# Two attentions on one core: the layout is told later landings for stacked keys and log-sum rows

## Chip, cores, metric

One Trainium2 chip, one core. The time is device microseconds of one execution; the number shown is the median of several executions. One execution was also taken by the hardware profiler, and the views quoted below come from that one.

## What is computed

Two attention blocks, each with its own input, weights and output projection, on sequences of 2048 positions with 1024 features, 32 heads of 32. B looks back over a dense window of 256 keys; A over 8 keys at distance 2. Cut to what matters:

```python
def _A_ref(x, wqkv, wo):          # W, dil = 8, 2
    q, k, v = split_heads(x @ wqkv)
    idx = pos[:, None] - arange(8)[None, :] * 2
    logits = einsum("bhsd,bhswd->bhsw", q, gather(k, idx)) * Dh ** -0.5
    attn = softmax(where(idx >= 0, logits, -1e9))
    return merge(einsum("bhsw,bhswd->bhsd", attn, gather(v, idx))) @ wo

def _B_ref(x, wqkv, wo):          # W = 256
    q, k, v = split_heads(x @ wqkv)
    scores = einsum("bhqd,bhkd->bhqk", q, k) * Dh ** -0.5
    mask = (i - j >= 0) & (i - j < 256)
    return merge(einsum("bhqk,bhkd->bhqd", softmax(where(mask, scores, -1e9)), v)) @ wo

return concatenate([A, B], axis=-1)
```

The positions of A are sorted into even and odd ones before the launch, so that its 8 keys at distance 2 are 8 neighbours.

## The kernel before

**Units and head groups.** The work is cut into 8 units of 512 positions: four of B (dense), then four of A (window). Each unit has 8 head groups of four heads, so there are 64 head groups, which the code numbers hg. For each head group the kernel computes queries and keys (L412, three matmuls of 512 columns for each of 8 slices of the contraction), for each pair of head groups values (L464, 256 columns), and for each unit the output projection (L510). Every projection is three matmuls per slice because each factor is split into a high and a low part; a weight tile arrives by a 512 KB load (L137, on GpSimd's queue after the first few) and DVE splits it with one cast (L163) and two subtractions (L171).

**Attention of a head group.** The query and key tiles are evacuated from PSUM in a high part (ACT, L349) and a low part (DVE, L353), into one of three `nat` buffers. SyncE copies both parts, stacked three deep, into `qst` and `kst` (L373: two copies of the high part and one of the low for keys), of which there are two each. The *first pass* (L681, 16 matmuls) makes the scores, DVE takes the row maxima (L686), ACT the sum of exponentials (L691). From maxima and sums the *log-sum* of each row is made (L704 to L712), turned with one matmul (L720), copied out of PSUM (L724) and put by a small DMA into two extra rows of `qst` (L727). With these rows the *second pass* (L763 in dense units, L566 in window units) makes scores that are already normalised in the exponent; ACT exponentiates, masks are applied, and L810 or L607 multiplies with the values. When the last second-pass matmul of a head group has been put in, the head group after the next may be stacked into the same `qst` and `kst` (`free_keys`, L629).

**The order is a plan.** The kernel is written out instruction by instruction in the order in which it was planned, and each engine runs its own instructions in that order. The plan is made by a small model, the class `Clock` (L35), while the kernel is being written out. It keeps a time for each engine and for the DMA, with constants for each step. A copy by SyncE, for example, starts `LEAD` = 1.34 us after its issue, moves for the first and ends after the second number of its kind in `MOVE` (`copy`: 1.18 and 0.56; `rows`: 0.37 and 0.56), and transfers follow one another in one lane.

There are four lists of items for TensorE: `aux` (the turn of the log-sums), `twos` (second pass and values), `ones` (first pass) and `gemm` (all projections). The loop at the end (L872) asks the next item of each list when it is ready, takes the one that can start first, with that order of lists where several are ready, and advances TensorE's clock by the item's cost. A projection item is one slice of the contraction: three matmuls of 512 columns, or six of 256. What an item triggers on other engines is put in when the clock reaches its time, so the order on ACT, DVE, GpSimd and SyncE follows from the same walk.

The two times that matter here are `done["stack"]`, the time at which the clock has the low keys of a head group stacked (L361), read by the first pass's items alone (L734), and `h["rows"]`, at which it has the log-sum rows in place (L728), read by the second pass's items alone (L793 and L620). On the chip these instructions wait on the semaphores of the real transfers, whatever the clock said.

Of the kernel before, what the change touches and what calls it, by code (L numbers as in the profile page):

```python
# [21 lines left out]
NRAW, NP, NO, NS = 3, 768, 10, 4  # L22
POOL_BIAS = -99
MASK_BIAS = 0.2
VPARTS = ((0,2),(2,2),(4,2),(6,2))
V_SLOTS = {0: 0, 1: 1, 5: 2, 7: 3}
O_SLOTS = {2: (0, 1), 3: (2, 3), 4: (4, 5), 5: (6, 7)}
V0_SLOTS = {0:0,2:1,4:2,7:3}
NX, NST, NN = 9,1,3
TAIL, XAT = 4, 1  # L30
C1, C3, CG, CV = 0.108, 0.2, 0.231, 0.242
TERMS = ((0, 0), (0, 1), (1, 0))
# [148 lines left out]
def kernel(ctx, tc, xs, wqk, wv, wo, outs, units):  # L181
# [19 lines left out]
    ck = Clock()  # L201
# [28 lines left out]
    for p in plan:  # L230
# [3 lines left out]
        elif p[0] == "v":  # L234
            s0, n = VPARTS[p[2]]
            for g in range(n):
# [55 lines left out]
    pfree = [0.0]  # L292
    vbuf = [const.tile([P, 6, n * P], F32, name=f"vbuf{i}") for i, (_, n) in enumerate(VPARTS)]
    vpart = {s0 + i: (p, i * P) for p, (s0, n) in enumerate(VPARTS) for i in range(n)}
    halo = [[dram.tile([P, 2, 256], F32, name=f"halo{i}_{s}") for s in range(NG)] for i in range(2)]

    xt, xready, ot = {}, {}, {}
    done, waiting = {}, {}
# [30 lines left out]
    def latest(*ts):  # L329
        return None if any(t is None for t in ts) else max(ts)  # L330


    def qk_items(u, s):
        out = []
        dense, has_halo = units[u][2], units[u][3]
        buf = s % 2
        hg = u * NG + s

        def read_halo():
            w = 256 if dense else 128  # L340
            hb = halo[(u + 1) % 2][s]
            for r, a in enumerate((0, 1, 0)):
                nc.sync.dma_start(kst[buf][r:96:3, :, 256 - w:256].bitcast(F32), hb[:, a, 256 - w:])
                ck.copy("halo_in" if dense else "halo_few", ck.now)

        def evac(t, ps, bank):
            hl = natp.tile([P, 2, S], F32R, tag="nat", name="nat")
            sc = SCALE if t == 0 else 1.0
            nc.scalar.activation(hl[:, 0, :], ps, AF.Copy, scale=sc)  # L349
            r = ck.use("act", 0.485, ck.now + ck.SEM)  # L350

            def low():
                nc.vector.scalar_tensor_tensor(hl[:, 1, :], ps, sc, hl[:, 0, :].bitcast(F32), op0=ALU.mult,  # L353
                                               op1=ALU.subtract)
                e = ck.use("dve", 0.61, r)
                rg.give(bank, e)

                def stack():
                    e2 = place(1, e)
                    if t == 1:  # L360
                        done["stack"][u, s] = max(e2, h2["hi"])  # L361
                    if t == 1 and u + 1 < U and units[u + 1][3]:
                        nc.sync.dma_start(halo[u % 2][s], hl[:, :, 256:].bitcast(F32))
                        e2 = ck.copy("halo_out", e, ck.now)
                    done["nat"][hg, t] = max(e2, h2["hi"])

                later(stack)

            def place(part, e):
                dst, c = (qst[buf], 0) if t == 0 else (kst[buf], 256)  # L370
                for i, a in enumerate((0, 0, 1) if t == 0 else (0, 1, 0)):
                    if a == part:
                        nc.sync.dma_start(dst[i:96:3, :, c:c + S].bitcast(F32), hl[:, a, :].bitcast(F32))  # L373
                        e2 = ck.copy("copy", e, ck.now)
                return e2

            def stack_hi():
                if t == 0 and has_halo:
                    read_halo()
                h2["hi"] = place(0, r)  # L380

            def later(f):
                if hg < 2 or hg - 2 in done["second"]:
                    f()
                else:
                    waiting.setdefault(hg - 2, []).append(f)

            h2 = {}
            later(stack_hi)
            ck.defer(r, low)  # L390

        for t in range(2):
            h = {}

            def ready(k, t=t, h=h):
                if k == 0:
                    st.split_to(where["qk", u, s, t] + 1)
                    h["w"] = st.ready[where["qk", u, s, t]]
                    return latest(rg.when(), h["w"], xready[u][0])
                if k >= len(xready[u]):  # L400
                    return None
                if k == NK - 1 and 2 * hg + t >= NN:
                    n = done["nat"].get(divmod(2 * hg + t - NN, 2))
                    return n and max(xready[u][k], n - 0.6)
                return xready[u][k]

            def run(k, t=t, h=h):
                if k == 0:
                    h["ps"], h["b"] = rg.take()
                    h["w"], _ = st.get(where["qk", u, s, t])  # L410
                for i, (a, b) in enumerate(TERMS):
                    nc.tensor.matmul(h["ps"], h["w"][:, a, k * P:(k + 1) * P], xt[u][k][:, b, :],  # L412
                                     start=(k == 0 and i == 0), stop=(k == NK - 1 and i == 2))
                if k == 3 and st.items[min(where["qk", u, s, t] + 1, len(st.items) - 1)][0] != "x":
                    st.split_to(where["qk", u, s, t] + 2)

            def after(k, t=t, h=h):
                if k == NK - 1:
                    evac(t, h["ps"], h["b"])

            for k in range(NK):
                out.append((lambda k=k, ready=ready: ready(k), lambda k=k, run=run: run(k), 3 * CG,
                            lambda k=k, after=after: after(k)))
        return out
# [11 lines left out]
    def v_items(u, part):  # L436
# [3 lines left out]
        h = {}  # L440
        s0, ng = VPARTS[part]
        nb, per = ng, 4 // ng
# [92 lines left out]
    def x_items(u):  # L535
        xt[u], xready[u] = [], []

        def run(g):
            a, b = st.get(where["x", u, g])
            xt[u] += a  # L540
            xready[u] += b

        return [[(lambda: 0.0, lambda g=g: run(g), 0.0, lambda: None)] for g in range(4)]
# [112 lines left out]
    def attention(u, s):  # L656
# [6 lines left out]
        h = {"left": 16, "rows": None}  # L663
# [54 lines left out]
        def rows(hl):  # L718
            ps, bank = rs.take()
            nc.tensor.matmul(ps[0:32, 0:P], hl.rearrange("p a b -> p (a b)"), cst["ident"], start=True, stop=True)  # L720
            rt = small.tile([32, P], F32R, tag="rt", name="rt")

            def copy():
                nc.vector.tensor_copy(rt, ps[0:32, 0:P])  # L724
                e = ck.use("dve", 0.2, ck.now)
                rs.give(bank, e)
                nc.sync.dma_start(q[96:98, :, :].bitcast(F32), rt.bitcast(F32))  # L727
                h["rows"] = ck.copy("rows", e)  # L728

            return copy  # L730

# [14 lines left out]
        def keep(w, mask, n, m, step, base, chan, r):  # L746
            dur_p, dur_d = m * n / 960 + 0.13, m * n / 960 + 0.07
            if ck.ends("pool", dur_p, r) <= ck.ends("dve", dur_d, r, port=True) + MASK_BIAS:
                nc.gpsimd.affine_select(w, w, pattern=[[0, m], [step, n]], compare_op=ALU.is_ge, fill=0.0,  # L749
# [90 lines left out]
    for p in plan:  # L840
# [8 lines left out]
        elif p[0] == "v":  # L849
            new = v_items(p[1], p[2])  # L850
            if V_SLOTS.get(NG - 1) == p[2] and p[1] + 1 < U:
                m = 2 * VPARTS[p[2]][1]
                for g, x in reversed(list(enumerate(x_items(p[1] + 1)))):
# [89 lines left out]
```

## Time and profile before

| | |
|---|---|
| median of 3 runs | 1946.54 us (1946.42, 1946.54, 1950.07) |
| the profiled execution | 1951.22 us |
| its span, first to last instruction | 1949.5 us |
| mean granted TensorE clock | 0.995 |
| L412, query and key projection | 799.2 us busy, 3072 matmuls |
| L464, value projection | 411.8 us busy, 3072 matmuls |
| L510, output projection (one of its three forms) | 356.7 us busy, 1416 matmuls |
| L681, first pass | 232.6 us busy, 1024 matmuls |
| stack copies qst<-nat and kst<-nat | 192 each, 256 KB each |
| row copies qst<-rt | 64, 16 KB each |
| weight and input loads on GpSimd's queue | 126 + 64 + 62 + 28, 512 KB each |

Busy time of an engine is the union of its instructions' spans. A wait is idle time of an engine just before an instruction, put down to the semaphore that came last. The chain of waits is followed back from the last instruction. The timeline lists instructions of all engines in order of time, merged where they follow one another; its times are us from the span's start.

### The profile page before, as it was taken

How to read it: one execution, taken by the hardware profiler on the slowest of the kernel's cores; microseconds unless marked ns; L12 is line 12 of the kernel's file. 1: busy time of each engine (PE TensorE's matmuls, PEld its weight loads, DVE VectorE, ACT ScalarE, POOL GpSimd, SP SyncE). 2: the span in 40 equal slices, each digit the busy share in tenths (PEclk: the TensorE clock that was granted, in tenths of full speed). 3: DMA queues.
4: the chain of work that ended last, by engine and by line, in shares of the span. 5: the costliest groups of instructions: out<-in, count | busy, mean ns of one | idle time of the engine just before them, and what ended most of it. 6: DMA issues, size and time to landing. Idle time of an engine off the chain costs nothing. (4 is left out here: it accounts for less than half of the span.)

```text
span 1949.5 us, 35937 instructions
## 1 busy us (share of the span) xinstructions
PE 1904.4 (98%) x12608; PEld 1608.6 (83%) x12608; DVE 1261.6 (65%) x3733; ACT 960.6 (49%) x3136; POOL 375.8 (19%) x958
## 2 busy tenths in 40 slices
PE   8999999999999999999999999999999999999999
PEld 6787787788877888778878888888888788888887
DVE  6667566667666676666755667656676566765673
ACT  3555565655565656565655333433444343434441
POOL 1222222323332323232431001000010000000010
PEclk9999999999999999999999999999999999999999
DMA  6456555455545464555454556545564556546451
GB/s 200 131 141 174 134 147 166 136 150 174 144 141 166 133 185 120 144 147 144 134 147 118 173 164 188 157 133 169 148 182 128 169 158 174 167 130 176 138 157 66
DMA packets 136500, 294.90 MB, mean 151 GB/s; under 512 B 14464, under 2 KB 42112, under 8 KB 136320
## 3 DMA queue, kind: packets, MB, share of 16 engines
q1 hardware_dynamic: 85632, 124.82, 26.0%
q0 software_dynamic: 40320, 146.82, 23.2%
q10 hardware_dynamic: 10368, 20.98, 3.0%
q8 instruction: 100, 1.64, 0.4%
q14 instruction: 80, 0.66, 0.1%
HBM read 163.58 MB, written 27.26 MB: 98 GB/s over the span
## 5 line engine op out<-in xcount | busy, mean ns | idle before, releaser
L412 PE MATMUL g<-x,w 128*128 128x512 f32 x3072 | 799.2, 398 | 9.3 <-DVE w L163 9.0
L412 PEld LDWEIGHTS g<-x,w 128*128 128x128 f32 x3072 | 556.9, 189 | 109.3 <-DVE w L163 10.2
L691 ACT ACTIVATE s<-s,nm 128x384 f32<-128x384 f32 (+3 forms) x1024 | 452.2, 442 | 269.1 <-DVE nm L686 261.0
L464 PE MATMUL g<-w,x 128*128 128x256 f32 x3072 | 411.8, 285 | 0.0
L464 PEld LDWEIGHTS g<-w,x 128*128 128x128 f32 x3072 | 392.9, 192 | 2.0 <-issue 0.2
L686 DVE CUSTOM_DVE_ANT_0 s<-s,mask_d 128x384 f32<-128x384 f32 (+2 forms) x512 | 262.4, 555 | 188.5 <-PE s L681 187.7
L510 PE MATMUL g<-ot,w 128*128 128x512 f32 x1416 | 356.7, 396 | 2.7 <-ACT ot L644 2.3
L171 DVE TENSOR_TENSOR w<-raw,w 128x512 fp32r<-128x512 f32 x502 | 328.0, 695 | 8.7
L510 PEld LDWEIGHTS g<-ot,w 128*128 128x128 f32 x1416 | 258.5, 189 | 53.6 <-ACT ot L644 3.3
L749 POOL TENSOR_SCALAR_AFFINE_SELECT pbuf<-pbuf 128x128 f32<-128x128 f32 (+1 forms) x643 | 219.0, 372 | 296.9 <-ACT pbuf L770 295.8
L681 PE MATMUL s<-kst,qst 96*128 96x384 f32 (+3 forms) x1024 | 232.6, 302 | 15.7 <-DMA kst<-nat 9.7
L770 ACT ACTIVATE pbuf<-s 128x384 f32<-128x384 f32 (+2 forms) x480 | 201.9, 503 | 65.8 <-PE s L763 62.6
L681 PEld LDWEIGHTS s<-kst,qst 96*128 96x128 f32 x1024 | 178.4, 190 | 55.6 <-issue 18.2
L686 DVE CUSTOM_DVE_ANT_0 s<-s,mask_w 128x136 f32<-128x136 f32 (+1 forms) x512 | 142.0, 321 | 113.2 <-PE s L681 112.8
L691 ACT ACTIVATION_READ_ACCUMULATOR s<-s,nm 128x1 f32 x1024 | 209.9, 205 | 0.0
L349 ACT ACTIVATE nat<-g 128x512 fp32r<-128x512 f32 x128 | 76.6, 599 | 249.7 <-PE g L412 245.4
L137 POOL DMA_DIRECT2D raw<-wqk x126 | 68.0, 540 | 572.7 <-DVE w L171 218.2
L353 DVE SCALAR_TENSOR_TENSOR nat<-g,nat 128x512 fp32r<-128x512 f32 x128 | 88.3, 690 | 139.1 <-ACT nat L349 136.2
L163 DVE CAST w<-raw 128x1024 fp32r<-128x1024 f32 x251 | 173.1, 690 | 7.3 <-DMA raw<-wqk 7.3
L686 DVE DVE_READ_ACCUMULATOR2_ANT nm<- 128x1 f32 x1024 | 143.7, 140 | 0.0
L763 PEld LDWEIGHTS s<-qst,kst 98*128 98x128 f32 x704 | 109.0, 189 | 40.4 <-ACT s L691 19.6
L583 DVE TENSOR_TENSOR pbuf<-pbuf,keep_w 128x272 f32<-128x272 f32 (+1 forms) x224 | 95.5, 471 | 70.1 <-ACT pbuf L573 69.8
(53 smaller groups left out, 1071.3 us busy)
## 6 DMA issues: line engine op xcount, KB each, us to landing
raw<-wqk POOLq DMA_DIRECT2D x126, 512.0 KB, 3.7
qst<-nat SPq DMA_DIRECT2D x192, 256.0 KB
kst<-nat SPq DMA_DIRECT2D x192, 256.0 KB
raw<-wo POOLq DMA_DIRECT2D x64, 512.0 KB, 3.7
raw<-wv POOLq DMA_DIRECT2D x62, 512.0 KB, 3.7
raw<-xs POOLq DMA_DIRECT2D x28, 512.0 KB, 4.7
outs<-ost ACTq DMA_DIRECT2D x56, 256.0 KB
halo<-nat SPq DMA_DIRECT2D x40, 256.0 KB
```

The costliest lines, as they stand in the source:

```text
L163: nc.vector.tensor_copy(t[:, 0, :], raw)
L171: nc.vector.tensor_tensor(o, a, b, op=ALU.subtract)
L412: nc.tensor.matmul(h["ps"], h["w"][:, a, k * P:(k + 1) * P], xt[u][k][:, b, :], start=(k == 0 and i == 0), stop=(k == NK - 1 and i == 2))
L464: nc.tensor.matmul(ps, xt[u][k][:, a, p0:p0 + P], h["w"][:, c, k % kw], start=(k == 0 and i == 0 and r == 0), stop=(k == NK - 1 and i == 2 ...
L510: nc.tensor.matmul(h["ps"], w[:, a, c:c + P], ot[u, k][:, b, :], start=(k == 0 and i == 0), stop=(k == NK - 1 and i == 2))
L583: nc.vector.tensor_tensor(w, w, cst["keep_w"][:, None, :n].to_broadcast([P, pack, n]), op=ALU.min)
L681: nc.tensor.matmul(ps[:, :n], q[0:96, j, b * P:(b + 1) * P], kk[0:96, j, c0:c1], start=True, stop=True)
L686: nc.vector.tensor_tensor_reduce(ps[:, :n], ps[:, :n], mask[:, cut:full], scale=-1.0, scalar=BIG, op0=ALU.add, op1=ALU.min, accum_out=nm)
L691: nc.scalar.activation(ps[:, :n], ps[:, :n], AF.Exp, bias=nm, scale=-1.0, accum_out=sm)
L749: nc.gpsimd.affine_select(w, w, pattern=[[0, m], [step, n]], compare_op=ALU.is_ge, fill=0.0, base=base, channel_multiplier=chan)
L763: nc.tensor.matmul(ps[:, i * n:(i + 1) * n], kk[0:98, j, 256 + kb * P:256 + (kb + 1) * P], q[0:98, j, q0:q0 + n], start=True, stop=True)
L770: nc.scalar.activation(w, ps[:, :pack * n].rearrange("p (j n) -> p j n", j=pack), AF.Exp)
```

## The change

Two constants are added, and each is added to one of the two times. One other line differs in spacing only.

```diff
+ROWS_LATE, KEYS_LATE = .4, .5
...
-NX, NST, NN = 9,1,3
+NX, NST, NN = 9, 1, 3
@@ def stack():
                     e2 = place(1, e)
                     if t == 1:
-                        done["stack"][u, s] = max(e2, h2["hi"])
+                        done["stack"][u, s] = max(e2, h2["hi"]) + KEYS_LATE
                     if t == 1 and u + 1 < U and units[u + 1][3]:
@@ def copy():
                 nc.sync.dma_start(q[96:98, :, :].bitcast(F32), rt.bitcast(F32))
-                h["rows"] = ck.copy("rows", e)
+                h["rows"] = ck.copy("rows", e) + ROWS_LATE
```

The clock's own account of SyncE and of the DMA is not touched: only the time that the items are told is later. `done["nat"]`, which tells the projections when a `nat` buffer is free, keeps its value.

## Prediction

> **What bounds the kernel now.** I read the page first, for the engine that is never free, then TensorE's own waits, then the chain and the timelines around those waits, last the granted clock by stretch.
>
> ```profile
> PE 1904.4 (98%) x12608; PEld 1608.6 (83%) x12608; DVE 1261.6 (65%) x3733; ACT 960.6 (49%) x3136; POOL 375.8 (19%) x958
> PE g L412 8%; PE g L510 6%; PE g L464 4%; PE s L566 1%; PE s L681 1%; PE o L607 1%; DMA qst<-rt 0%; DMA kst<-nat 0%; PE s L510 0%; DVE w L171 0%; DVE w L163 0%; DVE pbuf L583 0%; DVE s L686 0%; ACT s L691 0%; ACT nat L349 0%
> ```
>
> TensorE is busy 98% of 1949.5 us and leads the chain; the only transfers in the chain are the two that the diff names: the stacking of low keys (kst<-nat) and the row values (qst<-rt). TensorE's queue is in order, so the time is its matmul work plus the moments in which its next instruction is not ready. Of the 1949.5 us only 45.1 are not busy, and nothing in this diff removes a matmul. So it can only act on that remainder.
>
> TensorE's waits, in us in total, times, longest:
>
> ```profile
> PE s L681 <- DMA kst<-nat: 9.7, 6, 2.5
> PE g L412 <- DVE w L163: 9.0, 3, 8.1
> PE s L763 <- DMA qst<-rt: 5.3, 4, 1.8
> PE s L681 <- ACT s L691: 5.2, 5, 1.6
> PE s L566 <- DMA qst<-rt: 3.0, 3, 1.7
> ```
>
> Thirteen waits end with a landing that the layout expected earlier: six of the first pass for keys (9.7 us), seven of the second pass for rows (5.3 + 3.0 = 8.3 us), 18.0 us together, 0.9% of the span. The 8.1 us of L412 is the start, before any head group. One row wait and one key wait of the same two groups stand in the chain of waits between 1505 and 1545 us (start, us, what):
>
> ```profile
> 1510.39 4.47 DMA qst<-rt
> 1514.86 0.14 issue
> 1515.00 1.34 PE s L566 x10
> 1516.34 0.75 PE g L412 x3
> ...
> 1529.85 6.46 DMA kst<-nat
> 1536.30 0.09 issue
> 1536.39 0.63 PE s L681 x4
> 1537.03 1.44 PE g L510 x6
> ```
>
> The row transfer took 4.47 us from its issue, where the layout's clock computes 1.34 + 0.37 + 0.56 = 2.27 us plus what it believes is ahead in the DMA. TensorE stood 1.69 us in front of L566 (timeline), although L412 matmuls came right after, so projection work was there to be put ahead. That is so at all thirteen: in TensorE's timeline projection matmuls stand directly before each wait and within a few instructions after it. Where nothing collides the same transfer needs far less: in the timeline at 1736 us the rows' cast ends at 1735.76 + 0.28 = 1736.04 and L566 starts at 1739.74 with no wait shown, 3.70 us later; at 1510 us it was 4.64 us, and there GpSimd had issued a 512 KB load 0.08 us behind the rows' issue.
>
> **What the diff changes.** No instruction, no tile, no transfer is added or taken out. Two numbers that the layout compares with its clock grow: done["stack"] by 0.5 us, read only by the first pass's items, and h["rows"] by 0.4 us, read only by the second pass's. The layout's own queues (SP's above all) don't get longer. An attention item that would be due stays back 0.4 or 0.5 us, and projection items go first if they are ready. If none is ready the order stays, and the chip, which waits on real semaphores, does what it did: the lateness itself costs nothing on the chip. So the change is one of order alone.
>
> **The sum.** One projection item of three 512-wide matmuls occupies TensorE 0.74 us (chain: "PE g L412 x3" 0.75, elsewhere 0.74; one of six 256-wide ones 0.76). A due time that moves 0.4 us against a grid of 0.74 lets one more item in 0.4/0.74 = 54% of the cases, and 0.5 us in 68%: on the mean 0.4 and 0.5 us of real work are put into each wait.
>
> - Rows: seven waits, one by one from the timeline 1.80, 1.55, 0.74, 1.20, 0.65, 1.69, 0.67 us, all longer than 0.4. Taken 7 x 0.4 = 2.8 us off; bounds 0 (no item slips in) and one item each, 6 x 0.7 + 0.65 = 4.8.
> - Keys: 2.53, 1.92, 1.04, 2.04, 0.46, 1.70 us. Taken 5 x 0.5 + 0.46 = 3.0 off; bounds 0 and 5 x 0.7 + 0.46 = 4.0. The largest, 2.5 us, stays 2 us long: these waits are too long for 0.5 us to cover.
> - The other 57 row and 58 key landings had no wait. Putting an item ahead there is nothing in the sum while TensorE has later projection work; the cover is that work. Where it runs out, the item was spent early. One such place is seen, the last but one head group, around 1895 to 1900 us: TensorE waits 1.07, 0.37 and 0.71 us for ACT and DVE with no projection item left that does not need this group's output. There the chain of that group sets the time, and if its first and second pass each start late, its end is late by 0.5 + 0.4 = 0.9 us. Added: 0.9; bounds 0 and two items, 1.5.
> - What follows on other queues: the order on DVE, ACT, SP and POOL is written from the same walk. A first pass that comes later sends L686 to DVE behind a weight split (0.69 + 1.29 = 1.98 us), frees the keys later, and with that moves three 256 KB stack issues on SP and a 512 KB load on POOL. The trace of before cannot show the new neighbours. Bounds from the other stalls that exist now: TensorE's waits on ACT, 5.2 us in five, might shrink to 0 or double, so -5.2 to +5.2; I take 0, nothing in the rows says which side.
>
> Then the granted clock, by stretch (us, then PE, PEld, DVE, ACT, POOL busy, clock, DMA share, GB/s):
>
> ```profile
> 216.00:219.00 3.00, 1.70 (x13) 1.53 (x13) 2.30 (x6) 0.00 (x0) 0.52 (x1) 1.00 0.94 283
> 221.66:225.07 3.41, 3.41 (x18) 3.41 (x18) 2.40 (x10) 2.49 (x12) 0.00 (x0) 0.50 0.39 112
> 1044.27:1047.69 3.42, 3.42 (x18) 3.42 (x18) 1.34 (x11) 1.16 (x6) 0.00 (x0) 0.50 0.39 144
> 1221.76:1225.18 3.42, 3.42 (x11) 2.58 (x10) 2.40 (x6) 0.66 (x4) 0.11 (x1) 0.50 0.15 61
> 1897.60:1904.40 6.80, 5.73 (x39) 3.54 (x30) 2.74 (x11) 1.99 (x8) 0.00 (x0) 0.50 0.11 42
> ```
>
> After four clusters of waits the clock is 0.50, for 3.41 us three times and 6.8 us once. In such a stretch half the work is lost: 12 L464 matmuls took 2.50 us at 223 us, against 0.87 us for 6 at 225.7. Half of 3.41 is 1.7 us. Two of the four begin just after key waits, 1.92 us (matmul at 220.01) and 2.04 us (at 1043.68). Shortened by 0.5 us, each drop may or may not go: 0 to -3.4 us, taken -1.7; below zero saving too, since a new cluster can cost +1.7.
>
> The Trainium skill, "TensorE: Matmul & The Clock Gate", section "What's actually happening", says that the array falls to half clock after at least one idle window of about 3.4 us. The trace does not agree: no wait after the start is longer than 2.53 us, and the clock fell after one of 1.92. By the page there would be no such drops and this term would be 0, the sum -4.9 instead of -6.6; I go by the rows.
>
> Sum against the profiled execution: -2.8 - 3.0 + 0.9 - 1.7 = -6.6 us, 1951.2 (its time; span 1949.5) to 1944.6. That execution is 4.7 us above the median of the runs, 1946.54 (they lie at 1946.42, 1946.54, 1950.07). Drops of 1.7 us that come in some executions and not in others would make such a spread, so I don't take the clock term off the median: 1946.5 - 4.9 = **1941.6 us**. Everything at its good bound, -4.8 - 4.0 - 3.4 = -12.2, gives 1934.3.
>
> **Rivals.**
>
> *The collisions come back elsewhere.* Waits come where a copy shares the DMA with loads, and the new order meets loads at other groups. For it: the cast-to-use times of 4.64 and 3.70 us above differ by what the DMA carries, not by a constant; the DMA is about half busy all along (its digits on the page are 4 to 6). Against it: every group gets 0.4 and 0.5 us more margin, so the same collisions cost less. Time: -5.8 given back by as much, +0.9 for the end, 1946.5 to 1947.4; within 0.2%. The skill's "DMA: Bandwidth & Descriptors", "Issuing engines are not separate DMA queues", says that transfers from all queues interleave on the same 16 engines; the trace agrees with its 4.47 us of a 16 KB transfer beside a load.
>
> *Slower: the unit boundaries turn.* At the third dense boundary DVE, in order, stood 7.3 us at L163 for a late weight load, with L686 maxima behind it, ACT behind those, and TensorE behind ACT for PSUM banks. Between 975 and 1050 us TensorE waited 3.3 + 3.1 + 1.2 = 7.6 us, and lost 1.7 to the clock: 9.3. Around the two boundaries before it (455 to 545, 715 to 805) it waited 0.8 + 0.6 + 0.5 + 0.2 + 0.2 = 2.3 us each, the same waits in the same order, so the layout repeats itself there and both would turn together. Price 2 x (9.3 - 2.3) = +14.0, less 4.9: 1955.6 us. It decides from the point where both turn (one alone gives 1948.6). For it: a later first pass is just what puts maxima behind a split. Against: today two of three such boundaries pass, and 0.5 us is less than one item.
>
> *It does not do what it says:* the due time falls inside the same item at most of the thirteen waits, the order there stays, 1946.5 us.
>
> **How the numbers follow.** Forecast 0.47 (its own range 1936 to 1942.6), collisions back 0.26, boundaries 0.21, no effect 0.06. 0.2% is 3.9 us, which is about the spread of the runs shown and what a measurement can tell. Faster 0.47, same 0.32, slower 0.21. The range starts at 1935.5, just above the best bound, takes the same cases whole, and reaches to 1953 into the slower case, whose upper part is left out with some 0.15.
>
> **What would show it.** Right: the waits of L681 on kst<-nat fall from 9.7 to near 7 us and those of L763 and L566 on qst<-rt from 8.3 to near 5.5, with projection matmuls of L412, L464 or L510 in their place, all counts of instructions unchanged, and TensorE's idle time down from 45.1 to about 40. The clock term: no 0.50 after 220 and 1044 us. The end: waits between 1890 and 1901 us longer by up to 1.5. Wrong: the same totals on other groups (first rival), or L681 waiting on ACT and DVE on loads at the boundaries (second). A fall much beyond 12 us would mean that order does more than fill these thirteen waits.

## Result and profile after

| | before | after |
|---|---|---|
| median of the timed runs, us | 1947.35 (4 runs) | 1934.24 (4 runs, 1932.87 to 1938.99) |
| ratio, 95% interval | | 0.9935 [0.9915, 0.9955] |
| span of the profiled execution, us | 1949.5 | 1932.6 |

The change made the kernel faster, by more than was forecast: 13.1 us between the medians, against 4.9, and 1.3 us below the range. The ratio is the changed kernel's time over that of the kernel before, on the same chip. A second series with the same kernel (after_again below) gave 0.9919 [0.9905, 0.9933].

First the page of the changed kernel; its line numbers are one higher than before.

```profile
PE 1901.8 (98%) x12608; PEld 1608.3 (83%) x12608; DVE 1262.6 (65%) x3722; ACT 958.9 (50%) x3136; POOL 385.6 (20%) x969
```

The matmuls are the same 12608. DVE has 11 instructions fewer and GpSimd 11 more: the layout gave eleven masks to the other engine, as its queues now stood otherwise. TensorE is not busy for 1932.6 - 1901.8 = 30.8 us, against 45.1.

TensorE's waits in the changed kernel (us in total, times, longest):

```profile
PE g L413 <- DVE w L164: 8.6, 2, 8.2
PE s L682 <- ACT s L692: 4.2, 5, 1.8
PE s L682 <- DMA kst<-nat: 4.1, 4, 1.6
PE s L721 <- DVE hl L713: 2.4, 2, 2.0
PE s L764 <- DMA qst<-rt: 2.1, 4, 0.9
...
PE s L567 <- DMA qst<-rt: 0.2, 1, 0.2
```

The waits on row landings went from 8.3 us to 2.3, those on key landings from 9.7 to 4.1: 11.6 us less than the 18.0 that the prediction named. Below, "landing waits" are the sum of these two kinds.

How it looks at one place: head group 49, where L566 had waited 1.69 us behind 12 matmuls of L510 and 6 of L412. TensorE's timeline after (start, us, what):

```profile
1497.03 0.22 PE L721 MATMUL s<-ident,hl 128*32 128x128 f32 x1
1497.08 2.29 PE L511 MATMUL g<-ot,w 128*128 128x512 f32 x9
1499.21 2.88 PE L413 MATMUL g<-x,w 128*128 128x512 f32 x12
1501.94 1.27 PE L567 MATMUL s<-qst,kst 98*128 98x136 f32 x10
```

Between the turn of the log-sums and the second pass now stand 21 matmuls instead of 18, one item more (0.74 us), and no wait is marked. The item is not all that changed here. DVE, which runs its instructions in the order of the plan, copies the rows out of PSUM (L724, now L725). Before, it split a weight tile first; after, it copies first:

```profile
1508.16 0.69 DVE L163 CAST w<-raw 128x1024 fp32r<-128x1024 f32 x1
1508.88 1.29 DVE L171 TENSOR_TENSOR w<-raw,w 128x512 fp32r<-128x512 f32 x2
1510.09 0.27 DVE L724 CAST rt<-s 32x128 fp32r<-32x128 f32 x1
```

```profile
1497.28 0.28 DVE L725 CAST rt<-s 32x128 fp32r<-32x128 f32 x1 [0.92 <-PE s L721]
1497.49 0.67 DVE L164 CAST w<-raw 128x1024 fp32r<-128x1024 f32 x1
```

The copy starts 1.17 us behind the turn (1508.92) before and 0.25 us behind it (1497.03) after. The transfer behind it took 4.47 us from its issue before and 2.29 us after, by the updates of its semaphore. So 1.69 us of wait went where three things came together: 0.74 us of work, a copy 0.9 us earlier and a transfer 2.2 us quicker.

The clock, by stretch (us, then busy times, clock, DMA share, GB/s), for the places where it was 0.50:

```profile
180.48:183.89 3.41, 3.41 (x18) 3.41 (x18) 3.38 (x6) 0.60 (x1) 0.55 (x1) 0.50 1.05 204
1453.65:1457.06 3.41, 3.41 (x13) 2.83 (x12) 0.60 (x6) 2.00 (x9) 0.00 (x0) 0.50 0.00 1
1883.73:1887.14 3.41, 3.29 (x7) 2.39 (x8) 1.22 (x4) 1.36 (x8) 0.00 (x0) 0.50 0.00 0
```

These are 10.2 us at half clock instead of 17.1; a last stretch that begins as the work ends is left out of both. Half of such a stretch is lost work, so 3.4 us less are lost. So the span's 16.9 us are 14.3 of idle time and 3.4 of clock, with 0.8 the other way.

### The profile page after: what moved, and what is told of

Read it like the earlier page. It is cut to its first block, busy times and chain, and to the rows that moved or that the text cites. A ratio compares the mean times of both kernels' runs of the same rounds, so it can differ in the third digit from the quotient of the medians.

```text
span 1932.6 us, 35969 instructions
## 1 busy us (share of the span) xinstructions
PE 1901.8 (98%) x12608; PEld 1608.3 (83%) x12608; DVE 1262.6 (65%) x3722; ACT 958.9 (50%) x3136; POOL 385.6 (20%) x969
## 4 chain that ended last, share of the span: by engine, by line
PE 88%; DMA 4%; DVE 3%; issue 3%; ACT 1%; POOL 0%; SPq 0%; ACTq 0%; DVEq 0%; POOLq 0%
PE g L413 34%; PE g L465 17%; PE g L511 16%; PE s L682 7%; PE s L764 5%; PE o L811 4%; PE s L567 3%; DMA kst<-nat 2%; PE o L608 2%; DMA qst<-rt 1%; DVE w L172 1%; DMA raw<-xs 1%; DVE s L687 1%; ACT s L692 1%; DVE w L164 0%
## 5 line engine op out<-in xcount | busy, mean ns | idle before, releaser
L413 PE MATMUL g<-x,w 128*128 128x512 f32 x3072 | 799.1, 398 | 8.9 <-DVE w L164 8.6
L413 PEld LDWEIGHTS g<-x,w 128*128 128x128 f32 x3072 | 556.7, 189 | 108.8 <-DVE w L164 9.2
L750 POOL TENSOR_SCALAR_AFFINE_SELECT pbuf<-pbuf 128x128 f32<-128x128 f32 (+1 forms) x654 | 228.0, 379 | 288.9 <-ACT pbuf L771 287.1
L682 PE MATMUL s<-kst,qst 96*128 96x384 f32 (+3 forms) x1024 | 234.8, 301 | 10.2 <-ACT s L692 4.2
```

The lines of the kernel that those rows point to most:

```text
L682: nc.tensor.matmul(ps[:, :n], q[0:96, j, b * P:(b + 1) * P], kk[0:96, j, c0:c1], start=True, stop=True)
```

## Experiments

Theory M: the margin that the layout leaves in front of a landing is what empties these waits, each kind by its own number. Rival D: the old order was an unlucky draw of the layout's walk, and almost any other order would have lost such waits. The edits are against the changed kernel. Each ratio is to the kernel before on the same chip, whose median was 1950 to 1954 us there.

**One number at a time.**

```diff
-ROWS_LATE, KEYS_LATE = .4, .5
+ROWS_LATE, KEYS_LATE = 0.4, 0.0      # rows_only
+ROWS_LATE, KEYS_LATE = 0.0, 0.5      # keys_only
```

> Rows 0.4 us late, keys as before. Theory M (the margin itself empties the waits of its own kind): waits of the second pass on qst<-rt fall from 8.3 us to about 2 as in the changed kernel, those of the first pass on kst<-nat stay near 9.7; time about half of the way, 1940 to 1942. Theory D (the old order was an unlucky draw of the walk, and any other order loses such waits): both kinds of wait change by any amount, time anywhere from 1932 to 1946, not tied to the kind of wait.

> Keys 0.5 us late, rows as before. M: waits on kst<-nat fall from 9.7 to about 4, those on qst<-rt stay near 8.3; 1940 to 1942, and the two single gains add up to about 13 us. D: no tie between kind and wait; the two gains need not add up.

rows_only took 1942.67 us, ratio 0.9955 [0.9944, 0.9967]; keys_only 1947.28 us, 0.9979 [0.9970, 0.9988], beside 1951.02 for the kernel before on that chip. The waits, first of rows_only, then of keys_only:

```profile
PE s L682 <- DMA kst<-nat: 6.4, 5, 2.5
PE s L764 <- DMA qst<-rt: 2.2, 4, 0.8
```

```profile
PE s L764 <- DMA qst<-rt: 5.9, 5, 2.3
PE s L682 <- DMA kst<-nat: 5.1, 5, 1.5
PE s L567 <- DMA qst<-rt: 4.6, 7, 1.7
```

Each number took the waits of its own kind down (rows to 2.2, keys to 5.1). M had expected the other kind to keep its value, and it did not: keys fell to 6.4 with the rows' number alone, and rows rose to 10.5 with the keys' number alone. So for the keys these two runs do not tell their own number from a new order. The gains, 0.45% and 0.21%, add up to the 0.65% of both. In us they are 8.4 and 3.7, where M had about half of 13 for each: keys_only fell short.

**Other orders without lateness, and the same orders with it.** One constant of the layout is moved by a trifle, so that the walk comes out otherwise.

```diff
-C1, C3, CG, CV = 0.108, 0.2, 0.231, 0.242
+C1, C3, CG, CV = 0.108, 0.2, 0.232, 0.242                # ..._cg
-    SEEN = dict(act=0.15, dve=0.115, pool=0.08)
+    SEEN = dict(act=0.16, dve=0.115, pool=0.08)          # ..._seen
-ROWS_LATE, KEYS_LATE = .4, .5
+ROWS_LATE, KEYS_LATE = 0.0, 0.0                          # other_walk_...
```

> No lateness; the layout's cost of a projection matmul is 0.232 instead of 0.231 us, which gives the walk another order without more margin. M: waits on the two transfers stay near 18 us in total, time 1945 to 1949. D: those waits fall to 10 us or less, time 1932 to 1940.

> Both late as in the change, and the cost 0.232. M: waits on the two transfers 5 to 9 us in total, time within 3 us of the changed kernel, 1932 to 1938. D: nothing holds the waits down, time between 1934 and 1947, no nearer to the changed kernel than the walk without lateness is to the old one.

> A second walk without lateness: the layout's delay from ACT's end to its sight by others is 0.16 instead of 0.15 us. M2: landing waits 15 to 25 us in total, time within 20 us of before on either side. D (old order an unlucky draw): landing waits under 12 us and time under 1940.

> The same second walk with 0.4 and 0.5 us. M2: landing waits 8 to 14 us below those of the same walk without lateness, and a gain against it of 8 to 16 us. D: a gain of either sign.

| walk | ratio without lateness | ratio with it | landing waits, us | half clock, us |
|---|---|---|---|---|
| the kernel's own | 1 | 0.9935 [0.9915, 0.9955] | 18.0 to 6.4 | 17.1 to 10.2 |
| cg | 1.0078 [1.0061, 1.0094] | 1.0009 [0.9997, 1.0020] | 19.2 to 13.7 | 41.0 to 27.3 |
| seen | 1.0009 [1.0000, 1.0019] | 0.9919 [0.9904, 0.9934] | 20.4 to 5.0 | 23.9 to 23.9 |

D falls, but on less than three walks: without lateness all have 18 to 20 us of landing waits, and with it each gains, 0.65%, 0.69% and 0.90%. Of the two new orders without lateness, seen is hardly another one: as many projection matmuls as in the kernel before stand ahead of the rows in 57 of 64 head groups and ahead of the keys in 56, and 16.4 of its 20.4 us lie at the thirteen places of the prediction. cg is another order (27 and 36 groups the same): 9.1 us lie at those places and 10.1 at others. keys_only is a third for the rows, which have no lateness there (14 groups the same, 10.5 us). But a trifle in one constant is worth 0.8% by itself, as much as the change. So neither run of the walk cg came out where M had it: other_walk_cg took 1967.34 us, not 1945 to 1949, and late_other_walk_cg 1952.17 us with 13.7 us of landing waits, not 1932 to 1938 with 5 to 9. late_other_walk_seen went beyond: 15.4 us of landing waits fewer and 17.2 us faster than its walk without lateness, where 8 to 14 and 8 to 16 were expected. In the walk cg the clock carries as much as the waits: 41.0 us at half clock and 27.3 differ by 6.9 us of lost work, and the landing waits by 5.5.

**The dose.** Both numbers are scaled.

```diff
-ROWS_LATE, KEYS_LATE = .4, .5
+ROWS_LATE, KEYS_LATE = -0.4, -0.5    # early
+ROWS_LATE, KEYS_LATE = 0.2, 0.25     # half
+ROWS_LATE, KEYS_LATE = 0.8, 1.0      # double
+ROWS_LATE, KEYS_LATE = 1.6, 2.0      # quad
```

> Rows told 0.4 us and keys 0.5 us earlier than the clock computes. Theory M2 (landing waits follow the margin, rows more steeply than 0.4 us for each): rows' waits above 10 us, keys' above 10 us, 25 us or more together; time 1955 to 1970. Rival D2 (only some lucky order, the margin does not matter by itself): landing waits 10 to 20 us, time as likely below 1950 as above.

> Rows 0.2, keys 0.25 us late. M2: landing waits between those of the kernel before (18.0) and of the change (6.3), 10 to 15 us; time 1938 to 1948, give or take the walk's own scatter of some us. D2: anything.

> Rows 0.8, keys 1.0 us late. M2: rows' waits near 1 us, keys' 2 to 4, since the longest key wait was 2.5 us; time 1930 to 1938. A rival on the cost (each attention step that is held back is paid where projection work runs out): landing waits fall all the same, but waits on ACT and DVE rise by 4 us or more and the time is above that of the change.

> Rows 1.6, keys 2.0 us late. M2: landing waits under 2 us. If holding back is free, 1928 to 1936; if it is paid where projection work runs out, waits on ACT, DVE and PSUM above 15 us and the time above 1940.

| rows, keys late (us) | ratio, 95% interval | row waits | key waits | TensorE not busy | half clock |
|---|---|---|---|---|---|
| -0.4, -0.5 | 1.0102 [1.0077, 1.0128] | 12.9 | 12.0 | 52.0 | 34.1 |
| 0, 0 | 1 | 8.3 | 9.7 | 45.1 | 17.1 |
| 0.2, 0.25 | 0.9975 [0.9963, 0.9986] | 6.1 | 4.7 | 38.0 | 13.7 |
| 0.4, 0.5 | 0.9935 [0.9915, 0.9955] | 2.3 | 4.1 | 30.8 | 10.2 |
| 0.8, 1.0 | 0.9906 [0.9891, 0.9921] | 0.6 | 0.9 | 27.5 | 20.5 |
| 1.6, 2.0 | 0.9937 [0.9922, 0.9951] | 1.6 | 0 | 30.1 | 23.9 |

The landing waits fall with the dose, 24.9, 18.0, 10.8, 6.4, 1.5, 1.6 us, and the time with them up to twice the change's values, though the intervals of the change and of double overlap. (Waits of the first pass on another copy, kst<-halo, are not counted: 1.4 us in early and 1.7 in half.)

What the dose moves can be seen at the rows of all 64 head groups. The time from a row transfer's issue to its landing, by the updates of its semaphore, stays much the same: its median is 3.48 us before and after the change, and 21 and 18 of the 64 take over 4 us. What grows is the slack, from the landing to the moment when TensorE has done the work ahead. From early to quad its mean is 1.41, 1.87, 2.03, 2.13, 2.45 and 3.00 us.

In double the key waits fell to 0.9 us, under the 2 to 4 expected. Beyond it nothing is left to gain, and the price shows. The rival on the cost falls in double: TensorE's waits on ACT and DVE, without those of L413, are 12.6 us against the change's 10.6, not 4 more. In quad they are 15.7, as that rival had it, and 1937.88 us lies between the two times expected. Where quad pays is the end of the kernel. Its clock by stretch:

```profile
1877.29:1894.35 17.06, 15.66 (x92) 13.72 (x93) 9.15 (x26) 8.90 (x28) 0.45 (x2) 0.50 0.07 26
1894.35:1911.40 17.05, 17.05 (x111) 13.81 (x110) 5.92 (x11) 1.17 (x2) 1.07 (x2) 1.00 0.21 70
```

and its timeline of TensorE in the first of the two stretches:

```profile
1879.51 1.52 PE L567 MATMUL s<-qst,kst 98*128 98x8 f32 x6 [1.40 <-DMA qst<-rt]
1880.83 0.31 PE L721 MATMUL s<-ident,hl 128*32 128x128 f32 x1
1880.93 3.19 PE L567 MATMUL s<-qst,kst 98*128 98x136 f32 x14
1884.05 2.14 PE L608 MATMUL o<-pbuf,vbuf 128*32 128x8 f32 x40
1886.12 3.26 PE L567 MATMUL s<-qst,kst 98*128 98x8 f32 x14
```

The projections were put ahead, so the last groups' attention runs with hardly any of them between, at half clock for 17 us, of which 8.5 are lost. TensorE counts as busy for 92% of that stretch, and its waits there and in the two us before add up to 3.3 us. This is the cover of the prediction running out; in this one profile it costs less in idle time than in clock.

**The end without lateness.** The last three head groups get none.

```diff
-                        done["stack"][u, s] = max(e2, h2["hi"]) + KEYS_LATE
+                        done["stack"][u, s] = max(e2, h2["hi"]) + KEYS_LATE * (hg < 61)
-                h["rows"] = ck.copy("rows", e) + ROWS_LATE
+                h["rows"] = ck.copy("rows", e) + ROWS_LATE * (hg < 61)
```

> The change's 0.4 and 0.5 us for all head groups but the last three, which have none. If lateness is paid at the end (0.9 us was put into the sum for it), the waits behind 1875 us fall from 2.5 to about 1.6 us and the time is 1 us under the change's; if the end is indifferent, the time is the change's within 1 us.

> 0.8 and 1.0 us, none for the last three head groups. Theory (with twice the lateness the landing waits are gone, and what is left of its cost lies at the end, where three clock windows in a row were at half): the half-clock stretch near 1877 us falls from 10.2 to 3.4 or 6.8 us, time 1926 to 1930, under every kernel so far. Rival (the end costs the same however it is ordered): 1930 to 1933.

change_free_end: 1935.15 us, 0.9908 [0.9893, 0.9922]. Its interval overlaps the change's, and the waits of the last 75 us are 2.4 us, not the 1.6 that were expected, against 2.5; so whether the end matters at 0.4 and 0.5 us can't be told. double_free_end: 1929.18 us, 0.9874 [0.9859, 0.9888], within what was expected, against 0.9906 [0.9891, 0.9921] for double on another chip. Its half clock at 1877 us is 6.8 us instead of 10.2, but in a second profile of the same kernel, double_free_end_again, it is 3.4. One order varies by as much, so the clock at the end does not show what the free end is worth; the two times suggest a gain of about 2 us.

**Two sites, and the same orders again.** What remained was why the waits fell by twice what was taken.

```diff
-                        done["stack"][u, s] = max(e2, h2["hi"]) + KEYS_LATE
+                        done["stack"][u, s] = max(e2, h2["hi"]) + KEYS_LATE * (hg == 50)
-                h["rows"] = ck.copy("rows", e) + ROWS_LATE
+                h["rows"] = ck.copy("rows", e) + ROWS_LATE * (hg == 49)
```

> Rows 0.4 us late at head group 49 alone and keys 0.5 us late at head group 50 alone; in the order one projection item (three matmuls of L413) more stands ahead of that second pass, and everything before is as in the kernel before. If a wait is cut by the work that is put ahead of it: the wait of L567 near 1515 us falls from 1.69 to about 1.0 us, that of L682 near 1536 us from 1.70 to 1.0 or, with two items, 0.3. If lateness cuts more than it puts in: both near 0. The first twelve hundred us as before.

> The kernel before, profiled again. If the landing waits belong to the order: 18 us within 2, at the same places. If they are scatter of the execution: between 10 and 25 us.

> The changed kernel, profiled and timed again. If the waits belong to the order: 6.3 us within 2, and a ratio within 0.9915 to 0.9955. If they scatter: 3 to 15 us. The stretches at half clock, 10.2 us in the first profile, may differ between executions by a window of 3.4 us or more.

> 0.8 and 1.0 us late but for the last three groups, against the change on the same chip: 4 to 7 us faster than it, if the two ratios measured on different chips (0.9874 and 0.9935) hold.

TensorE's timeline at the two sites, first of the kernel before, then of two_sites (one execution, 1951.80 us):

```profile
1511.79 1.52 PE L412 MATMUL g<-x,w 128*128 128x512 f32 x6
1515.00 1.34 PE L566 MATMUL s<-qst,kst 98*128 98x136 f32 x10 [1.69 <-DMA qst<-rt]
...
1527.74 6.96 PE L510 MATMUL g<-ot,w 128*128 128x512 f32 x30
1536.39 0.63 PE L681 MATMUL s<-kst,qst 96*128 96x128 f32 x4 [1.70 <-DMA kst<-nat]
```

```profile
1513.79 2.20 PE L413 MATMUL g<-x,w 128*128 128x512 f32 x9
1516.66 1.34 PE L567 MATMUL s<-qst,kst 98*128 98x136 f32 x10 [0.67 <-DMA qst<-rt]
...
1528.70 8.32 PE L511 MATMUL g<-ot,w 128*128 128x512 f32 x36
1537.34 0.63 PE L682 MATMUL s<-kst,qst 96*128 96x128 f32 x4 [0.32 <-issue]
```

At the rows, three more matmuls stand ahead (9 for 6), 0.7 us of work, and the wait is 1.02 us shorter (0.83 against the 1.50 us that before_again had there). DVE's split stays ahead of the copy of the rows here, and 0.67 us of the wait stay too. At the keys, six more stand between the last key projection and the first pass (36 for 30), 1.4 us, and the wait is 1.38 us shorter. So where the rest of the order stays, the wait is cut by about the work that is put in, and that comes in whole items. The two items at the keys are not the keys' 0.5 us alone: when the layout writes the order out with only one of the two numbers, either one puts three matmuls more there (neither order was timed). It is one item for each number.

before_again has landing waits of 18.6 us (7.7 and 10.9) against 18.0, after_again 8.2 (4.1 and 4.1) against 6.4: in total they belong to the order, to within 2 us, and 14.9 of the 18.6 lie at the thirteen places. The half clock does not: 34.1 us against 17.1, and 13.7 against 10.2. after_again took 1937.64 us, double_free_end_again 1929.15 us, 0.9880 [0.9863, 0.9898], both beside 1952.46 for the kernel before. The last beats both kernels, the change by 8.5 us on one chip, where 4 to 7 were expected.

**An account of all profiles.** Take each profiled span, less TensorE's idle time, less half of its time at half clock. Before: 1949.5 - 45.1 - 8.5 = 1895.9. After: 1932.6 - 30.8 - 5.1 = 1896.7. Over all eighteen profiles, whose spans run from 1926.7 to 1966.5 us, it lies between 1893.8 and 1899.4. Idle time and clock are nearly all in which these orders differ.

## Why the prediction was right and wrong

*The bound and the kind of change: right.* TensorE's work stayed, the order alone moved, and the time went with the two kinds of wait named there. "All counts unchanged" missed the eleven masks that moved to GpSimd. Two readings were too wide: the chain before reaches back only to 1507 us, so what it holds is true of the last quarter, and at 1193 us the matmul right before the wait is one of the first pass, not a projection.

*"On the mean 0.4 and 0.5 us of real work are put into each wait": this step failed.* It gave 2.8 + 3.0 = 5.8 us, where the landing waits lost 11.6 (10.4 between the second two profiles): rows 6.0 for 2.8, keys 5.6 for 3.0. The sum shortened thirteen waits, each at its own place, and let the rest of the order stand. The order did not stand:

- At the thirteen places 18.0 us of waits became 3.0, and 3.4 us came up at places that had had none (5.1 in after_again): rows near 111, 304, 534 and 819 us, where the kernel before had no wait over 0.25.
- Over all 64 head groups the projection work between the turn of the log-sums and the second pass grew in 33 and shrank in 20. By the matmuls in TensorE's timeline, at 0.74 us for an item, it grew by 0.24 us on the mean. Between the last key projection and the first pass it grew in 34 and shrank in 16, by 0.09 us on the mean.
- Of the thirteen, five got just one item more (185, 1001, 1193, 1515 and 1536 us), and their waits went from 7.8 to 0.9 us for 3.7 us of work. Four got less work ahead and lost their waits all the same (196, 220, 1025 and 1680 us). One got 24 matmuls more and waited longer (1464 us, 0.46 to 1.60).

The thirteen were the groups for which the old order happened to turn out worst. A new order loses many of these waits whatever its margin, and draws others: cg without lateness kept 9.1 of the 18.0 us and drew 10.1. How many it draws is what the margin decides: as many as it lost without lateness, 3.4 us here with it. So the bounds "one item each", 4.8 and 4.0, were no bounds. That the gain came to twice the sum is in part the luck of this draw: the three walks lost 5.5, 11.6 and 15.4 us for the same numbers. The prediction's own sign for this, "a fall much beyond 12 us", was met by the 13.1.

*"I don't take the clock term off the median": this failed too.* The term was put at -1.7 us against the profile and at 0 against the median. Measured were -3.4 us between the first two profiles (half of 17.1 - 10.2), and -10.2 between before_again and after_again (half of 34.1 - 13.7). Single profiles vary, as was argued, but the granted clock of every run of the second series is on record, and there the median carries the term as well. The span times what is missing of the clock has a median of 11.7 us in eleven runs before and 6.8 in six after: 4.9 of the 14.8 us between the medians, to about 1 us, as the clock is given to three decimals. Half clock goes with waits, but not strictly: the nine profiles with the most idle time have 26.5 us of it on the mean, the nine with the least 15.2. What sets off a drop stays open.

*The end, +0.9 us: too small to be seen.* TensorE's waits behind 1875 us went from 2.2 to 2.5 us, and the half clock there from 6.8 to 3.4. At four times the dose the end did pay, more by half clock than by waits.

*The rivals.* The collisions did come back elsewhere, but with smaller waits: 3.4 and 5.1 us at new places, and in total 6.4 and 8.2 where this rival had 18. The unit boundaries did not turn to the worse; the third got better: between 970 and 1050 us the changed kernel's TensorE waits for 1.1 us, where before it waited 7.6 us from 975 to 1050.

The sum with every good bound, 12.2 us off, would have come close, but by luck: its terms count on the thirteen places.

## What to carry to other kernels

When a program's order is laid out against computed times, a landing that comes late stops the in-order engine, while one that is counted late costs nothing as long as other work is ready: in this kernel a margin on the two transfers that TensorE waited for paid up to the point where the filler runs out, about twice the change's values, with none for the last groups. Price such a margin over the whole population of landings and their slack, not wait by wait: the waits seen in one order are its worst draws, and a new order will not keep them. Price the clock with the waits, and compare a change with a few neutral reorderings, since an irrelevant constant moved this kernel by 0.8%.

## What was not expected of the hardware

TensorE falls to half clock without any long wait: after the start, the longest of TensorE's waits in the eighteen profiles is 2.6 us. In the changed kernel a wait of 1.60 us at 1452.82 was followed by 3.41 us at 0.50; in quad the clock stayed there from 1877 us on for 17.1 us, with no wait in that stretch or the two us before it over 1.44 us, while small attention matmuls ran almost alone. All stretches at half clock, in eighteen profiles, are 3.41 us or a multiple of it, but for those that begin as the work ends. The Trainium skill, "TensorE: Matmul & The Clock Gate", section "What's actually happening", has a window of 3.4 us, and the trace agrees; it puts the fall behind at least one idle window, and here the trace does not agree.

Executions of one order differ by this more than by their waits: 17.1 and 34.1 us at half clock for the kernel before, with 45.1 and 43.8 us of idle time.
